# Attention followed by a gated token mixer on one core: TensorE's work regrouped into longer stretches of one kind, and its eight PSUM banks shared out anew

## The chip, the core and the metric

The kernel runs on one core of one Trainium2 chip. The metric is the device time of one execution in microseconds, of which three were taken before the change: 924.58, 922.16 and 916.06, with a median of 922.16. A lower time is better.

## What is computed

The reference has two parts. The first is attention with a sliding window, for 8 sequences of 576 tokens with 8 heads of 64 channels. The second is a token mixer on the 512 channels of all heads together. Cut to what matters:

```python
scores = scale * np.matmul(q, k.transpose(0, 1, 3, 2))          # (8, 8, 576, 576)
mask = (rel >= 0) & (rel < 128)                                  # rel = query - key
scores = np.where(mask, scores + slope[h] * -np.abs(rel), -1e9)
attn = softmax(scores)
x = heads_side_by_side(np.matmul(attn, v))                       # (8, 576, 512)

theta = x @ w_theta
zr, zi = x * np.cos(theta), x * np.sin(theta)
y = w_tok_r @ zr + w_tok_i @ zi                                  # mixes the tokens
u = x + y
out = u + np.maximum(u @ w_ch, 0.0)
```

## The kernel before

**Precision.** Most products are made of two or three TensorE products: an operand is split into a rounded high part and a remainder (the names end in h and l, or hi and lo), and high·high, high·low and low·high add up in one PSUM tile.

**Attention** works on pairs of heads (`Pair`, 32 of them, four for each sequence). A pair's scores come in three tiles, `scores((0, 2))`, `scores((3, 4))` and `scores((1,))` (line 271; the numbers are blocks of query rows). TensorE's part (line 285) is 12, 12 and 6 matmuls in which the two heads use 64 rows of the array each, so that two run side by side; they write one PSUM tile `s_ps` of two banks. VectorE adds the bias to it and takes the row's least value (line 292, 4, 4 and 2 times), which empties the tile into `s_sb`. ScalarE makes the exponential (line 296).

A head (`Head`, line 299) then goes through two steps per half, called bank 0 (query blocks 0, 2 and 1) and bank 1 (blocks 3 and 4). `flip(bank)` turns the exponentials over on TensorE (line 316, five or four transposes into one PSUM tile `t_ps`), and ScalarE and VectorE split the result into two fp16 parts `pt` (lines 362 and 363). `values(bank)` multiplies it with v (line 333, 15 and 12 products for the two banks, each 128x65 or 128x64 in fp16, into `acc`). `finish` (line 336) divides by the sum and writes the head's columns of `x_sb`.

**The mixer** follows for each sequence in three parts, written as generators whose parts can be taken one at a time. `turn` (line 366) goes over five blocks of tokens: `columns` transposes x (line 386), splits it and keeps a copy in `xtf` (lines 397 to 399). `products` multiplies with w_theta (line 406, 12 matmuls of 512 columns, 8 for the last block), and `angle` makes cosine and sine (lines 420 to 428), multiplies with x (430, 432) and splits the result into `z_hi` (line 377, ScalarE) and `z_lo` (line 378, GpSimd). `mix` (line 452) makes the eight pieces of y, each 27 matmuls of 288 columns (line 465), yielding after every three; VectorE adds the piece to `xtf` (line 470). `channels` (line 476) makes the last product, eight pieces of 12 matmuls (line 485) and the rectified sum (line 488). All PSUM tiles of the mixer come from one pool, under the name `mm`.

**What sets the order.** `attend` (line 518) runs the attention of sequence b+1 while `other`, the mixing of sequence b, is handed out in steps of three matmuls between its parts: 18 steps per pair, four pairs. The order in which `attend` calls things is only a first word, though. The program is then scheduled by priorities and a timeline of its own, which moves instructions on each engine; within an engine they run in the order that results. The first 96 us or so are `start` (line 561): the first sequence's attention, with the weights being unpacked beside it. After the last sequence's attention there is a mixer with no attention beside it.

**PSUM** has eight banks, shared among four pools (lines 63 to 66): `s_ps` two buffers of two banks each, `t_ps` one, `acc` one, `mm` two.

**Values.** `load_values` (line 189) fetches v of four heads and takes its largest absolute value on VectorE at once (line 197); `spread_scales` (line 202) makes a power of two of it.

Of the kernel before, what the change touches and what calls it, by code (L numbers as in the profile page):

```python
# [11 lines left out]
F32 = mybir.dt.float32  # L12
# [8 lines left out]
B, H, S, D = 8, 8, 576, 64  # L21
DM = H * D
NT = 5
# [13 lines left out]
GROUP = 4  # L37
# [9 lines left out]
def attn_moe_kernel(ctx: ExitStack, tc: tile.TileContext, qt, kt, vx, wth, wtok, wch, band, out):  # L47
    nc = tc.nc
    PSUM = bass.MemoryType.PSUM
# [5 lines left out]
    vbp = ctx.enter_context(tc.tile_pool(name="vbp", bufs=2))  # L55
# [4 lines left out]
    tp = ctx.enter_context(tc.tile_pool(name="tp", bufs=2))  # L60
    uf = ctx.enter_context(tc.tile_pool(name="uf", bufs=2))
    big = ctx.enter_context(tc.tile_pool(name="big", bufs=1))
    ps_s = ctx.enter_context(tc.tile_pool(name="ps_s", bufs=2, space=PSUM))
    ps_t = ctx.enter_context(tc.tile_pool(name="ps_t", bufs=1, space=PSUM))
    ps_a = ctx.enter_context(tc.tile_pool(name="ps_a", bufs=1, space=PSUM))
    ps_m = ctx.enter_context(tc.tile_pool(name="ps_m", bufs=2, space=PSUM))

    class Ring:

# [117 lines left out]
    group_v = {}  # L187

    def load_values(g):

        b, h = divmod(GROUP * g, H)
        vb = vbp.tile([128, GROUP, NT, 65], F32, name="vb")
        nc.sync.dma_start(out=vb, in_=vx[b, h:h + GROUP].rearrange("h p (c d) -> p h c d", d=65))
        most = rings["most"].take()
        nc.vector.tensor_reduce(out=most, in_=vb[:, :, :, :64], axis=mybir.AxisListType.XY, op=ALU.max,
                                apply_absolute_value=True)
        nc.vector.tensor_scalar(out=most, in0=most, scalar1=2.0 ** -100, scalar2=None, op0=ALU.max)
        group_v[g] = vb, most  # L200

    def spread_scales(g):
        vb, most = group_v[g]
        m_ps = ps_m.tile([128, 512], F32, name="mm")
        nc.tensor.transpose(m_ps[:GROUP, :128], most, ident)
        whole = rings["whole"].take()
        nc.vector.tensor_reduce(out=whole[:GROUP, :1], in_=m_ps[:GROUP, :128], axis=mybir.AxisListType.X, op=ALU.max)
        spread = rings["vs"].take()
        nc.vector.tensor_scalar(out=spread[:GROUP], in0=ident[:GROUP, :GROUP], scalar1=whole[:GROUP, :1],
                                scalar2=None, op0=ALU.mult)  # L210
        w_ps = ps_m.tile([128, 512], F32, name="mm")
        nc.tensor.matmul(w_ps[:, :GROUP], ones[:GROUP].broadcast_to([GROUP, 128]), spread[:GROUP],
                         start=True, stop=True)
        scale = rings["scale"].take()
        nc.vector.tensor_scalar(out=scale.bitcast(I32), in0=w_ps[:, :GROUP].bitcast(I32), scalar1=0x7F800000,
                                scalar2=None, op0=ALU.bitwise_and)
        nc.vector.tensor_scalar(out=scale.bitcast(I32), in0=scale.bitcast(I32), scalar1=-1.0,
                                scalar2=float((2 * 127 + VEXP) << 23), op0=ALU.mult, op1=ALU.add)
        group_v[g] = vb, scale
# [40 lines left out]
    class Pair:  # L260
# [10 lines left out]
        def scores(self, tiles, behind=None):  # L271

            ps = ps_s.tile([128, 2, 512], F32, name="s_ps")
            sbs = [sp.tile([128, len(tiles), 128 if tiles == (1,) else 256], F32, name=f"s_sb{len(tiles)}")
                   for _ in range(2)]
            if 0 in tiles:

                for sb in sbs:
                    nc.gpsimd.memset(sb[:64, 0, 192:], 0.0)  # L279
            for k, i in enumerate(tiles):  # L280
                q0, qn, k0, kn, c0 = TILES[i]
                for j, (qm, km) in enumerate(self.terms):
                    for e in range(2):
                        rows = slice(64 * e, 64 * e + 64)
                        nc.tensor.matmul(ps[:qn, e, 256 * k:256 * k + kn], qm[rows, q0:q0 + qn], km[rows, k0:k0 + kn],  # L285
                                         start=(j == 0), stop=(j == len(self.terms) - 1))
            for k, i in enumerate(tiles):
                _, qn, _, kn, c0 = TILES[i]
                for e in range(2):
                    sb = sbs[e][:qn, k, :kn]  # L290
                    least = self.mx[:qn, e, i:i + 1]
                    nc.vector.tensor_tensor_reduce(out=sb, in0=ps[:qn, e, 256 * k:256 * k + kn],  # L292
                                                   in1=bnd[:qn, c0:c0 + kn], scale=2.0 ** -((2 * self.p + e) % H + 1),
                                                   scalar=3.0e38, op0=ALU.add, op1=ALU.min, accum_out=least)
                    with tc.issue_after(behind.ins) if behind is not None else nullcontext():
                        self.exp = nc.scalar.activation(sb, sb, AF.Exp, bias=least, scale=-1.0)  # L296
                    self.heads[e].sc[i] = sbs[e][:qn, k]
# [196 lines left out]
    pairs = B * H // 2  # L494
# [9 lines left out]
    def step(stream, k=1):  # L504
        for _ in range(k):
            next(stream, None)
# [11 lines left out]
    def attend(b, x_sb, other, first, behind):  # L518

        for g in range(H // 2):  # L520
            p = b * H // 2 + g
            one, two = first.pop(0).heads
            new = None
            if p + DEPTH < pairs:
                new = Pair(p + DEPTH)
                first.append(new)

            def scores(tiles):
                if new is not None:
                    new.scores(tiles, behind)  # L530

            one.flip(0)
            step(other)
            scores((0, 2))
            step(other, 2)
            one.flip(1)
            step(other, 3)
            one.values(0)
            two.flip(0)
            step(other, 3)  # L540
            one.values(1)
            one.finish(x_sb)
            if new is not None:
                new.heads[0].ready()
            scores((3, 4))
            step(other)
            two.flip(1)
            step(other, 2)
            if p % 2 == 0 and p + 2 < pairs:
                spread_scales(p // 2 + 1)  # L550
            scores((1,))
            two.values(0)
            prepare(p + DEPTH + 2)
            step(other, 4)
            two.values(1)
            two.finish(x_sb)
            if new is not None:
                new.heads[1].ready()
            step(other, 2)

    def start(x_sb, load):

        paces = [0]

        def pace(k=1):
            for _ in range(k):
                paces[0] += 1
                if paces[0] * 3 % 5 < 3:
                    next(load, None)

        for p in range(2):
            prepare(p)
        last = None
        for p in range(H // 2 + 1):
            new = Pair(p) if p < H // 2 else None
            if new is not None:
                for head in new.heads:
                    head.ready()

            def scores(tiles):  # L580
                if new is not None:
                    new.scores(tiles)
                pace(2 * len(tiles))

            if last is not None:
                one, two = last.heads
                one.flip(0)
                one.flip(1)
                scores((0, 2))
                two.flip(0)  # L590
                one.values(0)
                one.values(1)
                one.finish(x_sb)
                scores((1,))
                two.flip(1)
                scores((3, 4))
                two.values(0)
                two.values(1)
                two.finish(x_sb)
            else:  # L600
                for tiles in SCORES:
                    scores(tiles)
            if new is not None:
                prepare(p + 2)
            last = new
        for _ in load:
            pass
# [31 lines left out]
    x_sb = xp.tile([128, NT, DM], F32, name="x_sb")  # L639
    start(x_sb, unpack(JOBS, ((big, "u_hi"), (big, "u_lo"), (uf, "xtf"), (uf, "xtf"))))  # L640
    for p in range(H // 2, H // 2 + DEPTH):
        load_values(p // 2)
        spread_scales(p // 2)
        first.append(Pair(p))
        for head in first[-1].heads:
            head.ready()
        for tiles in SCORES:
            first[-1].scores(tiles)
        prepare(p + 2)
    st[0]["exp"] = first[-1].exp  # L650
    rotated(turn(x_sb, st[0]), iter(()))
    for b in range(B):
        chans = urgent(channels(b, st[b]), CHAN if b else CHAN0)
        mixing = urgent(mix(st[b]), MIX if b else MIX0)
        other = ahead(mixing, chans) if b else ahead0(mixing, chans)
        if b + 1 < B:
            x_sb = xp.tile([128, NT, DM], F32, name="x_sb")
# [56 lines left out]
```

## Time and profile before

| | |
|---|---|
| median of three runs | 922.16 us |
| the profiled execution's own time | 919.67 us |
| its span, first to last instruction | 917.9 us |
| mean granted TensorE clock | 0.933 |
| TensorE busy (matmuls) | 797.7 us, 87% |
| VectorE, ScalarE, GpSimd busy | 62%, 53%, 29% |
| DMA | 49.65 MB, mean 54 GB/s |

The profile is of one execution. A group's row gives the busy time and the mean duration of one instruction. TensorE's matmuls are pipelined, so that the duration of one is longer than the time after which the next may start; what a matmul costs in a stream is the distance between the starts of two neighbours. An engine's instructions start in their order, so one that waits holds up all behind it. The order and the waits of one sequence's period come again in the next ones, so that one period of the middle can be read for all of them.

### The profile page before, as it was taken

The numbers are of one execution on the slowest core, as the hardware profiler recorded it, in microseconds if no ns is written. First come the engines' busy times: TensorE is split into PE (matmuls) and PEld (weight loads), VectorE is DVE, ScalarE is ACT, GpSimd is POOL, SyncE is SP. The second block draws the span as 40 slices with busy tenths as digits, with TensorE's granted clock in tenths as the row PEclk, the third lists the DMA queues.
The fourth block names the chain that finished last, engine by engine and source line by source line (L and its number), as shares of the span: only waits on it lengthen the run. The fifth ranks groups of instructions, "written<-read, shape, count | busy, mean of one in ns | idle before, by whom it ended". The sixth has DMA issues, their size and how long they took to land.

```text
span 917.9 us, 16440 instructions
## 1 busy us (share of the span) xinstructions
PE 797.7 (87%) x6338; PEld 694.8 (76%) x6338; DVE 566.7 (62%) x1535; ACT 488.2 (53%) x962; POOL 269.1 (29%) x324
## 2 busy tenths in 40 slices
PE   3669867999989888998889889898889988897898
PEld 3558656987878777887778778787678877796798
DVE  5897697565655765656755766556656567443522
ACT  5556467545664466544664456544674356632620
POOL 5773164211412233220422213121332105110331
PEclk9999886997989999999989989899989989798999
DMA  5541311021110210111110211112110210000001
GB/s 207 181 145 41 117 59 53 27 69 40 52 30 27 94 47 22 54 57 46 52 37 27 72 39 50 31 44 84 46 43 27 68 40 27 1 1 21 26 8 52
DMA packets 29550, 49.65 MB, mean 54 GB/s; under 512 B 2592, under 2 KB 19104, under 8 KB 29472
## 3 DMA queue, kind: packets, MB, share of 16 engines
q1 hardware_dynamic: 29472, 48.61, 16.5%
q8 instruction: 50, 0.82, 0.4%
q14 instruction: 28, 0.23, 0.1%
HBM read 39.16 MB, written 9.44 MB: 53 GB/s over the span
## 4 chain that ended last, share of the span: by engine, by line
PE 57%; DVE 16%; ACT 15%; DMA 6%; issue 3%; POOL 3%; ACTq 0%; SPq 0%; DVEq 0%; POOLq 0%
PE mm L465 20%; PE mm L406 10%; PE mm L485 8%; PE s_ps L285 6%; PE t_ps L316 6%; ACT s_sb L296 5%; PE acc L333 4%; DMA vb<-in_vx_dram 4%; DVE s_sb L292 2%; DVE g L423 2%; DVE f L421 2%; ACT z_hi L377 2%; ACT g L427 1%; DVE pt L363 1%; DMA xtf<-in_wch_dram 1%
## 5 line engine op out<-in xcount | busy, mean ns | idle before, releaser
L465 PE MATMUL mm<-wtk_hi,z_hi 128*128 128x288 f32 x576 | 180.4, 315 | 19.0 <-ACT z_hi L377 15.5
L465 PE MATMUL mm<-wtk_hi,z_lo 128*128 128x288 f32 x576 | 175.4, 311 | 0.6 <-POOL z_lo L378 0.4
L465 PE MATMUL mm<-wtk_lo,z_hi 128*128 128x288 f32 x576 | 174.9, 306 | 0.0
L292 DVE CUSTOM_DVE_ANT_0 s_sb<-s_ps,fixed 128x256 f32<-128x256 f32 (+2 forms) x320 | 108.5, 376 | 71.7 <-PE t_ps L316 63.7
L296 ACT ACTIVATE s_sb<-s_sb,fixed 128x256 f32<-128x256 f32 (+2 forms) x320 | 127.7, 465 | 14.0 <-DVE fixed L292 13.8
L465 PEld LDWEIGHTS mm<-wtk_hi,z_hi 128*128 128x128 f32 x576 | 111.4, 194 | 25.6 <-ACT z_hi L377 17.0
L316 PE MATMUL t_ps<-fixed,s_sb 128*128 128x128 f32 (+1 forms) x576 | 106.8, 304 | 24.9 <-DVE pt L363 9.2
L362 ACT ACTIVATE pt<-t_ps 128x512 f16<-128x512 f32 x112 | 66.8, 596 | 110.1 <-PE t_ps L316 109.3
L465 PEld LDWEIGHTS mm<-wtk_hi,z_lo 128*128 128x128 f32 x576 | 110.4, 194 | 5.1 <-POOL z_lo L378 3.5
L465 PEld LDWEIGHTS mm<-wtk_lo,z_hi 128*128 128x128 f32 x576 | 111.7, 194 | 1.5
L316 PEld LDWEIGHTS t_ps<-fixed,s_sb 128*128 128x128 f32 (+1 forms) x576 | 71.6, 156 | 40.5 <-ACT s_sb L296 10.8
L378 POOL TENSOR_TENSOR z_lo<-g,z_hi 128x512 fp32r<-128x512 f32 x40 | 53.0, 1326 | 140.0 <-ACT z_hi L377 140.0
L472 POOL TENSOR_TENSOR u_lo<-xtf,u_hi 128x288 fp32r<-128x288 f32 x64 | 53.6, 841 | 121.5 <-ACT u_hi L471 121.5
L333 PE MATMUL acc<-vh,pt 128*128 128x65 f16 x1008 | 82.4, 204 | 5.7 <-ACT pt L362 4.7
L333 PEld LDWEIGHTS <-pt 128*128 128x128 f16 x1512 | 70.7, 104 | 17.6 <-ACT pt L362 7.0
L363 DVE SCALAR_TENSOR_TENSOR pt<-t_ps,pt 128x512 f16<-128x512 f32 x112 | 76.2, 680 | 7.9 <-ACT pt L362 7.5
L285 PE MATMUL s_ps<-kh,qh 64*128 64x256 f32 (+2 forms) x320 | 61.8, 356 | 18.7 <-DVE fixed L292 10.8
L333 PE MATMUL acc<-vl,pt 128*128 128x64 f16 x504 | 70.5, 202 | 0.0
L285 PE MATMUL s_ps<-kh,ql 64*128 64x256 f32 (+2 forms) x320 | 55.8, 320 | 11.6 <-DVE ql L227 11.6
L230 POOL TENSOR_TENSOR kl<-kr,kh 128x576 fp32r<-128x576 f32 x32 | 49.1, 1535 | 56.5 <-ACT kh L229 51.2
L285 PEld LDWEIGHTS s_ps<-kh,qh 64*128 64x128 f32 (+1 forms) x320 | 35.7, 203 | 37.2 <-DVE fixed L292 14.6
L279 POOL MEMSET s_sb<- 64x64 f32 x64 | 9.1, 146 | 185.1 <-PE t_ps L316 185.1
(111 smaller groups left out, 1610.7 us busy)
## 6 DMA issues: line engine op xcount, KB each, us to landing
vb<-in_vx_dram SPq DMA_DIRECT2D x16, 650.0 KB, 4.3
qr<-in_qt_dram SPq DMA_DIRECT2D x32, 288.0 KB, 3.1
kr<-in_kt_dram SPq DMA_DIRECT2D x32, 288.0 KB, 2.9
out_dram<-xtf SPq DMA_DIRECT2D x64, 144.0 KB, 1.8
xtf<-in_wtok_dram SPq DMA_DIRECT2D x4, 576.0 KB, 4.6
xtf<-in_wch_dram SPq DMA_DIRECT2D x4, 512.0 KB, 3.8
u_hi<-in_wtok_dram SPq DMA_DIRECT2D x3, 576.0 KB, 3.9
u_lo<-in_wtok_dram SPq DMA_DIRECT2D x2, 576.0 KB, 5.0
```

Of the source, the lines that this page charges most:

```text
L285: nc.tensor.matmul(ps[:qn, e, 256 * k:256 * k + kn], qm[rows, q0:q0 + qn], km[rows, k0:k0 + kn], start=(j == 0), stop=(j == len(self.terms ...
L292: nc.vector.tensor_tensor_reduce(out=sb, in0=ps[:qn, e, 256 * k:256 * k + kn], in1=bnd[:qn, c0:c0 + kn], scale=2.0 ** -((2 * self.p + e) % ...
L296: self.exp = nc.scalar.activation(sb, sb, AF.Exp, bias=least, scale=-1.0)
L316: nc.tensor.transpose(t_ps[:, off:off + w], self.sc[i][:, 128 * j:128 * j + 128], ident[:w, :w])
L333: nc.tensor.matmul(av[:, i, :r.shape[-1]], l, r, start=(n == 0), stop=(n == len(prods) - 1))
L362: nc.scalar.activation(pt[:, 0], t_ps, AF.Copy, scale=2.0 ** PEXP)
L363: nc.vector.scalar_tensor_tensor(out=pt[:, 1], in0=t_ps, scalar=2.0 ** PEXP, in1=pt[:, 0], op0=ALU.mult, op1=ALU.subtract)
L378: nc.gpsimd.tensor_tensor(out=z_lo[:, c, :], in0=z, in1=z_hi[:, c, :].bitcast(F32), op=ALU.subtract)
L406: nc.tensor.matmul(t_ps, a[:, c * 128:c * 128 + 128], w[:, c, :], start=(k == 0 and c == 0), stop=(k == len(prods) - 1 and c == 3))
L465: nc.tensor.matmul(y_ps[:, :HALF], z[:, c, m * 128:m * 128 + 128], w[:, c, cs], start=(k == 0), stop=(k == 26))
L472: nc.gpsimd.tensor_tensor(out=u_lo[:, m, cs], in0=xtf[:, m, cs], in1=u_hi[:, m, cs].bitcast(F32), op=ALU.subtract)
L485: nc.tensor.matmul(o_ps[:, :HALF], w[:, c, e * 128:e * 128 + 128], u[:, c, cs], start=(k == 0), stop=(k == 11))
```

## The change

Four things are done.

1. In `attend`, both `flip` calls of a head stand together, both `values` calls of a head stand together, and the 18 mixing steps of a pair come as three parts of six instead of eight parts of one to four. `scores((1,))` moves behind the second head's `finish`.
2. The PSUM pools: `s_ps` goes from two buffers to one (four banks to two), `t_ps` from one to two, `mm` from two to three; `acc` keeps one. That is eight banks again.
3. `load_values` is cut in two: it only fetches, and the new `measure` takes the largest value later. `attend` calls `measure` in the second third of every other pair, and `spread_scales` later than before.
4. In `start`, one fetch of values is issued a pair earlier, since the pairs before the main loop need it measured.

```diff
-    ps_s = ctx.enter_context(tc.tile_pool(name="ps_s", bufs=2, space=PSUM))
-    ps_t = ctx.enter_context(tc.tile_pool(name="ps_t", bufs=1, space=PSUM))
+    ps_s = ctx.enter_context(tc.tile_pool(name="ps_s", bufs=1, space=PSUM))
+    ps_t = ctx.enter_context(tc.tile_pool(name="ps_t", bufs=2, space=PSUM))
     ps_a = ctx.enter_context(tc.tile_pool(name="ps_a", bufs=1, space=PSUM))
-    ps_m = ctx.enter_context(tc.tile_pool(name="ps_m", bufs=2, space=PSUM))
+    ps_m = ctx.enter_context(tc.tile_pool(name="ps_m", bufs=3, space=PSUM))
...
         nc.sync.dma_start(out=vb, in_=vx[b, h:h + GROUP].rearrange("h p (c d) -> p h c d", d=65))
+        group_v[g] = vb
+
+    def measure(g):
+        vb = group_v[g]
         most = rings["most"].take()
         nc.vector.tensor_reduce(out=most, in_=vb[:, :, :, :64], axis=mybir.AxisListType.XY, op=ALU.max,
...
             one.flip(0)
-            step(other)
+            one.flip(1)
             scores((0, 2))
-            step(other, 2)
-            one.flip(1)
-            step(other, 3)
+            step(other, 6)
             one.values(0)
-            two.flip(0)
-            step(other, 3)
             one.values(1)
             one.finish(x_sb)
             if new is not None:
                 new.heads[0].ready()
+            two.flip(0)
+            two.flip(1)
             scores((3, 4))
-            step(other)
-            two.flip(1)
-            step(other, 2)
+            if p % 2 == 0 and p + 2 < pairs:
+                measure(p // 2 + 1)
+            step(other, 6)
+            two.values(0)
+            two.values(1)
+            two.finish(x_sb)
+            scores((1,))
             if p % 2 == 0 and p + 2 < pairs:
                 spread_scales(p // 2 + 1)
-            scores((1,))
-            two.values(0)
             prepare(p + DEPTH + 2)
-            step(other, 4)
-            two.values(1)
-            two.finish(x_sb)
             if new is not None:
                 new.heads[1].ready()
-            step(other, 2)
+            step(other, 6)
...
+            if p == 3:
+                load_values(2)
...
-        load_values(p // 2)
+        measure(p // 2)
```

What the scheduler makes of it shows in the built programs. All lines from `measure` on stand four further down in the changed file (285 becomes 289, and so on). Taking a stretch to be TensorE instructions of one line in a row, the stretches are these:

| TensorE line (before) | instructions | stretches before | stretches after |
|---|---|---|---|
| 285, scores | 960 | 158, of which 38 hold a single matmul | 133, none of a single matmul |
| 316, transposes of a head | 576 | 138 | 141 |
| 333, products with v in fp16 | 1512 | 180, of which 7 hold a whole head's 27 | 87, of which 33 hold 27 |
| 465, mixing | 1728 | 151 | 151 |
| 485, channels | 768 | 63 | 81 |
| 406, angles | 448 | 40 | 45 |
| all lines | | 818 | 713 |

Two places show what the sums below rest on. The first is TensorE in the middle of the mixing, where a pair's last score tile, `scores((1,))`, is made. `s_ps` is its PSUM tile, `mm` is the mixer's, `t_ps` the transposes'. Before:

```order
L316 MATMUL t_ps<-fixed,s_sb_5394 128x128
L285 MATMUL s_ps<-kh,qh 128x128
L465 MATMUL mm<-wtk_hi,z_hi 128x288
L285 MATMUL s_ps<-kh,qh 128x128
L465 MATMUL mm<-wtk_lo,z_hi 128x288
L285 MATMUL s_ps<-kh,ql 128x128
L465 MATMUL mm<-wtk_hi,z_lo 128x288
L285 MATMUL s_ps<-kh,ql 128x128
L285 MATMUL s_ps<-kl,qh 128x128 x2
L465 MATMUL mm<-wtk_hi,z_hi 128x288
```

After the change, the same tile of a pair:

```order
L337 MATMUL acc<-vh,pt 128x65
L289 MATMUL s_ps<-kh,qh 128x128 x2
L289 MATMUL s_ps<-kh,ql 128x128 x2
L289 MATMUL s_ps<-kl,qh 128x128 x2
L216 MATMUL mm<-fixed 128x4
L320 MATMUL t_ps<-fixed,s_sb_5491 128x64 x2
L320 MATMUL t_ps<-fixed,s_sb_5491 128x128 x2
L469 MATMUL mm<-wtk_hi,z_lo 128x288
```

The two heads' matmuls stood apart with one mixing matmul between them; now they stand in pairs, and the tile is one stretch.

The second place is VectorE where it empties a tile `scores((0, 2))`, `s_ps`, into `s_sb` (each emptying has a second row that writes the least value to `fixed`). Before:

```order
L292 ISA s_sb_4995,fixed<-s_ps,fixed 64x192
L292 ISA fixed 64x1
L363 SCALAR_TENSOR_TENSOR pt<-t_ps,pt 128x512
L339 TENSOR_SCALAR fixed<-acc,fixed 128x5
L341 RECIPROCAL fixed<-fixed 128x5
L246 SCALAR_TENSOR_TENSOR vl<-vb,fixed,vh 128x320
L342 TENSOR_TENSOR x_sb<-acc,fixed 128x5x64
L292 ISA s_sb_4996,fixed<-s_ps,fixed 64x192
L292 ISA fixed 64x1
L292 ISA s_sb_4995,fixed<-s_ps,fixed 128x256
L292 ISA fixed 128x1
L292 ISA s_sb_4996,fixed<-s_ps,fixed 128x256
```

After the change, the same tile:

```order
L367 SCALAR_TENSOR_TENSOR pt<-t_ps,pt 128x512 x2
L296 ISA s_sb_4995,fixed<-s_ps,fixed 64x192
L296 ISA fixed 64x1
L296 ISA s_sb_4996,fixed<-s_ps,fixed 64x192
L296 ISA fixed 64x1
L296 ISA s_sb_4995,fixed<-s_ps,fixed 128x256
L296 ISA fixed 128x1
L296 ISA s_sb_4996,fixed<-s_ps,fixed 128x256
L296 ISA fixed 128x1
```

The emptying of a tile was spread around the work on a head's result; now its four parts stand in a row, behind the work on both of a head's transposed tiles.

## The prediction, made before the changed kernel ran

> **What bounds the kernel now.** I read the page first: busy times, and the chain that ended last.
>
> ```profile
> PE 797.7 (87%) x6338; PEld 694.8 (76%) x6338; DVE 566.7 (62%) x1535; ACT 488.2 (53%) x962; POOL 269.1 (29%) x324
> PE 57%; DVE 16%; ACT 15%; DMA 6%; issue 3%; POOL 3%; ACTq 0%; SPq 0%; DVEq 0%; POOLq 0%
> ```
>
> TensorE is the engine to look at, and the chain leaves it for VectorE and ScalarE in a third of the span: TensorE is short of time and also waits. Next, the stretches view, for one sequence's period in the middle (length, then busy time and count of TensorE, weight loads, VectorE, ScalarE, GpSimd, then the granted clock).
>
> ```profile
> 352.40:458.40 106.00, 95.83 (x803) 82.67 (x803) 66.46 (x186) 58.78 (x118) 26.50 (x38) 0.95 0.15 47
> ```
>
> A period is 106 us. Seven of them fill nearly all of the span behind the start. TensorE's 95.83 us busy isn't 95.83 us of use, since a matmul's duration contains its passage. So I read its timeline by the distance between starts.
>
> ```profile
> 400.83 0.29 PE L465 MATMUL mm<-wtk_hi,z_hi 128*128 128x288 f32 x1
> 400.96 0.29 PE L465 MATMUL mm<-wtk_lo,z_hi 128*128 128x288 f32 x1
> ...
> 401.17 0.38 PE L465 MATMUL mm<-wtk_hi,z_lo 128*128 128x288 f32 x1
> 401.39 0.29 PE L465 MATMUL mm<-wtk_hi,z_hi 128*128 128x288 f32 x1
> 401.61 0.33 PE L285 MATMUL s_ps<-kh,qh 64*128 64x128 f32 x2
> 401.78 0.27 PE L285 MATMUL s_ps<-kh,ql 64*128 64x128 f32 x2
> 401.89 0.28 PE L285 MATMUL s_ps<-kl,qh 64*128 64x128 f32 x1
> ...
> 402.17 0.19 PE L333 MATMUL acc<-vl,pt 128*128 128x64 f16 x1
> 402.20 0.22 PE L333 MATMUL acc<-vh,pt 128*128 128x65 f16 x2
> ...
> 402.50 0.81 PE L316 MATMUL t_ps<-fixed,s_sb 64*128 64x64 f32 x5
> 403.24 0.33 PE L285 MATMUL s_ps<-kl,qh 64*128 64x128 f32 x1
> 403.50 0.40 PE L465 MATMUL mm<-wtk_lo,z_hi 128*128 128x288 f32 x1
> 403.74 0.29 PE L465 MATMUL mm<-wtk_hi,z_lo 128*128 128x288 f32 x1
> ```
>
> In a stream a mixing matmul takes 0.13 us (400.83 to 400.96), a pair of scores 0.11 (401.78 to 401.89), a product with v 0.03 (402.17 to 402.20), five transposes 0.74. Leaving one kind for another costs on top. Behind two products with v, the first mixing matmul holds the next back to 0.22 us instead of 0.13 (401.17 to 401.39): 0.09. From mixing to scores it is 0.22 (401.39 to 401.61): 0.09 again. Behind scores the first mixing matmul takes 0.24 (403.50 to 403.74): 0.11. The dearest form is scores one at a time between mixing matmuls:
>
> ```profile
> 276.48 0.32 PE L285 MATMUL s_ps<-kh,qh 64*128 64x128 f32 x1
> 276.74 0.40 PE L465 MATMUL mm<-wtk_lo,z_hi 128*128 128x288 f32 x1
> 277.06 0.32 PE L285 MATMUL s_ps<-kh,qh 64*128 64x128 f32 x1
> ```
>
> One score and one mixing matmul take 0.58 us here (276.48 to 277.06); in streams they take half of 0.11 and 0.13, 0.19 together. Each single score wastes 0.39 us.
>
> Last, who waits for whom on TensorE, over the five periods from 247.4 to 777.3 us (total, times, longest):
>
> ```profile
> PE mm L465 <- ACT z_hi L377: 11.3, 5, 2.3
> PE mm L485 <- DVE f L421: 6.9, 9, 1.2
> PE s_ps L285 <- DVE ql L227: 6.2, 6, 1.2
> PE t_ps L316 <- ACT s_sb L296: 5.1, 5, 1.0
> PE t_ps L316 <- DVE pt L363: 3.8, 11, 0.6
> PE acc L333 <- ACT pt L362: 3.7, 5, 0.8
> PE s_ps L285 <- DVE fixed L292: 3.4, 13, 0.7
> PE mm L406 <- ACT xtf L394: 2.5, 4, 0.7
> PE mm L406 <- ACT xtf L399: 2.4, 3, 1.1
> PE mm L485 <- ACT xtf L399: 1.1, 5, 0.2
> ```
>
> That is 46.4 us, over 9 us a period, and no wait leads by far. Several are waits for a PSUM buffer rather than for data: lines 421, 394 and 399 are the last readers of an `mm` tile, 363 of `t_ps`, 292 of `s_ps`.
>
> **The change part by part.** (1) Fewer changes of kind. The 38 single scores become none: 38 x 0.39 = 14.8 us less. The other stretches of scores go from 120 to 133; one costs 0.09 to enter and some 0.2 to leave (0.11 and about 0.1 at its last pair), so 13 x 0.3 = 3.9 more. The counted orders have mixing behind products with v 56 times before and 13 now, 43 x 0.09 = 3.9 less; but mixing behind transposes 16 times before and 51 now. At the same 0.09, which I take since both are followed by the same matmul, that is 3.2 more. Channels and angles alternate more often (63 and 40 stretches become 81 and 45), with no price of its own in the rows above; from nothing to 2 us, I take 1 more. Sum: -14.8 + 3.9 - 3.9 + 3.2 + 1 = -11.6, call it **-11** (bounds -15 and -7). It lies on TensorE, with nothing beside it. The mixing is not in longer stretches at all, 151 before and after: the scheduler spends the parts of six again.
>
> The Trainium skill (TensorEngine Tiling (Array Packing), Key Properties) says that changing the tiling mode drains TensorE. By that rule only the 64-row scores would cost, 25 stretches fewer with two changes each at 0.09, 4.5 us, and the sum would come out 6.5 us later. The trace agrees at 401.61 and goes further: at 401.17 a change costs as much where both kinds use 128 rows.
>
> (2) Transposes ahead, two `t_ps`. With both flips of a head together and a second buffer, the transposes need not wait for line 363, and the products with v come a whole head behind the transposes, so that line 362 is done. The two rows are 3.8 + 3.7 = 7.5 us in five periods, 1.5 each, 10.5 in seven. I take **-9** (bounds -10.5 and -5). VectorE's and ScalarE's work for `pt` is the same; it is late for nobody, since other TensorE work stands between.
>
> (3) A third `mm` tile. The four rows of lines 421, 394 and 399 make 12.9 us in five periods, 18 in seven. A third buffer helps where the buffer is all that is missing; where the same ScalarE and VectorE work must deliver data next, the wait only moves. I take half, 9. The last mixer, without attention beside it, shows the wait alone (waits from 835 to 872 us, then TensorE's timeline):
>
> ```profile
> PE mm L485 <- DVE f L421: 3.5, 3, 1.4
> PE mm L485 <- ACT xtf L399: 1.8, 1, 1.8
> ```
>
> ```profile
> 849.70 0.80 PE L485 MATMUL mm<-u_hi,wch_hi 128*128 128x288 f32 x4 [0.97 <-DVE f L421]
> ```
>
> Channels, angles and transposes alternate there, with the same order after the change; with two tiles, the channels' tile is that of the angles before, still being read. The third removes that: 3.5 of the 5.3 us. Together **-12.5** (bounds -23 and -4).
>
> (4) Scores wait less for `ql`. Six waits, 6.2 us. In the new order two of a period's four such places have 25 mixing matmuls or a head's products behind the first two scores. Half of 8.7 in seven periods: **-4** (bounds -8.7 and 0).
>
> (5) One `s_ps`. The next tile's scores must now wait until VectorE has emptied the last one. In the trace of before, a tile's last scores and the emptyings that follow:
>
> ```profile
> 388.77 0.28 PE L285 MATMUL s_ps<-kl,qh 64*128 64x256 f32 x2
> ```
>
> ```profile
> 391.56 0.35 DVE L292 CUSTOM_DVE_ANT_0 s_sb<-s_ps,fixed 64x192 f32<-64x192 f32 x1 [2.44 <-PE t_ps L316]
> ...
> 397.24 0.46 DVE L470 TENSOR_TENSOR xtf<-mm,xtf 128x288 f32<-128x288 f32 x1 [3.20 <-PE mm L465]
> ...
> 398.38 0.41 DVE L292 CUSTOM_DVE_ANT_0 s_sb<-s_ps,fixed 128x256 f32<-128x256 f32 x1
> 398.72 0.68 DVE L363 SCALAR_TENSOR_TENSOR pt<-t_ps,pt 128x512 f16<-128x512 f32 x1
> ```
>
> Ten microseconds pass before the tile is empty, but VectorE idles for 5.64 of them: it waits in its own queue, first for transposes that free an `s_sb` buffer, then for a mixing piece. In the new order the transposes come first and the four emptyings stand in a row: 4 x 0.41 = 1.6 us, behind at most two `pt` of 0.68, so 3.0 us. Between two tiles TensorE now has, for example, 14 mixing matmuls, nine transposes and 27 products with v: 1.8 + 1.3 + 0.8 = 3.9 us. It fits on average, with 0.9 to spare. The old wait of 0.7 a period (3.4 in five) may go, or grow where `finish` or a mixing piece stands ahead: I take 1 us more a period, **+7** (bounds -5 and +20).
>
> (6) The start, where VectorE is nearly the bound (17.87 of 20 us):
>
> ```profile
> 40.00:60.00 20.00, 10.56 (x57) 9.15 (x57) 17.87 (x32) 9.64 (x18) 16.49 (x11) 1.00 0.55 170
> ```
>
> One `s_ps` lets less be made ahead of it, but TensorE has half of the time free: **+2** (bounds -3 and +8). Fetching values apart from measuring them takes a DMA wait from VectorE and moves no TensorE work; VectorE is not the bound there, so nothing. The wait of 11.3 us for `z_hi` stays, see the second rival.
>
> Sum: -11 - 9 - 12.5 - 4 + 7 + 2 = **-27.5 us** against the profiled execution's 919.67, so 892.2. That execution is 2.5 us below the median of the three runs (922.16); a median to be measured would be 894 to 895. I say **894**.
>
> **The rivals.** *A: the single score tile holds TensorE up.* If VectorE's own queue, without its idling, stays as long as in the rows above, a tile takes 10.0 - 5.6 = 4.4 us to empty. The shorter places between tiles hold 16 mixing matmuls, four transposes and 27 products with v, 2.1 + 0.6 + 0.8 = 3.5 us, so 0.9 us is missing. For the 56 large tiles of seven periods that is 50 us in place of the 7 above: -34.5 + 50 = +15.5, **938**, slower. It decides from 34.5/56 = 0.6 us a tile. For it: VectorE runs strictly in its order. Against it: the four emptyings stand together now. The Trainium skill speaks for this rival (Perfetto Trace Analysis, Matmuls): independent groups should rotate through different PSUM banks, so that emptying one overlaps the next one's matmuls. The change follows that for the mixer and drops it for the scores; the trace has not shown a single tile yet.
>
> *B: the saved waits come back at the next one.* The mixing's last products need `z_hi` of the last tokens, which stands on ScalarE behind 15 exponentials:
>
> ```profile
> 357.90 5.56 ACT L296 ACTIVATE s_sb<-s_sb,fixed 64x192 f32<-64x192 f32 x15
> ...
> 363.37 0.60 ACT L377 CAST z_hi<-g 128x512 fp32r<-128x512 f32 x1
> ```
>
> The new order still has 14 there. If the way through ScalarE and VectorE sets the period, what (2), (3) and (4) save is waited for there: -27.5 + 25.5 = -2, **920**. Against it: ScalarE is busy for 58.78 of 106 us.
>
> *C: the third tile gives all, and the clock with it.* The granted clock is 0.95 over a period; if the rest is at half speed, that is 10.6 us, which cost 5.3. Fewer waits could win half back, 18 us in seven periods, and the `mm` waits another 10.5: -27.5 - 28.5 = -56, **866**.
>
> **How the numbers follow.** My forecast has 0.55, with its own range 875 to 913; A 0.12, B 0.18, C 0.15. The range 864 to 924 takes in B, my own and most of C and leaves out A. A change of 1% is about what a measurement of this kernel can tell from none: 913 and 931 are the marks. Nearly all of my forecast and C are faster, 0.70; B is the same, 0.18; A slower, 0.12.
>
> **What would show it.** TensorE: single scores between mixing matmuls are gone; the waits of line 316 for 363 and of 333 for 362 are under 1 us a period; those for 421, 394 and 399 are about halved, and in the last mixer the 0.97 us is gone. The wait of the scores for the emptying (line 292, then 296) tells (5): under 2 us a period is my forecast, 6 or more is A. The wait for `z_hi` grown from 2.3 to 5 us or more a period is B. A granted clock of 0.97 in a period is C. A period of 102 us is right for the whole; 106 or more is wrong.

## The result: 803.8 us, and where 116 us went

The changed kernel takes 803.77 us (median of four runs, 802.54 to 803.89); the kernel before took 920.12 with a fourth run added. The ratio is 0.872, 95% interval 0.868 to 0.876. Faster was forecast, but 894 us, and the range ended at 864: the gain is four times the one predicted.

The profile after is read in the same order as the one before. First the page: busy times and the chain that ended last.

```profile
PE 740.5 (92%) x6338; PEld 656.0 (82%) x6338; DVE 567.2 (71%) x1535; ACT 481.8 (60%) x962; POOL 260.6 (32%) x324
PE 60%; DVE 16%; ACT 15%; issue 4%; DMA 3%; POOL 1%; SPq 0%; ACTq 0%; DVEq 0%; POOLq 0%
```

VectorE and ScalarE do the same work in nearly the same time as before (567 and 482 us). TensorE's 6338 matmuls are the same too, but it is busy 57 us less: the same matmuls then took less time each, or overlapped more. The clock line of the page stands in tenths for 40 slices; first before, then after.

```profile
PEclk9999886997989999999989989899989989798999
```

```profile
PEclk9999999799999999999999999999999999999999
```

Before, the granted clock fell twice in each of the five periods that the prediction read; after, it fell only between 138 and 162 us, around the beginning of the first mixing. The page's mean was 0.933 and is 0.991. The trace's clock record knows only full and half speed; half speed takes 124 us of it before, 2 x (1 - 0.9327) x 917.9, and 14 after. That leaves out the time ahead of the record, which comes below with the start.

Next the stretches: the five periods that the prediction read (530 us before), then one of them.

```profile
244.90:679.60 434.70, 430.86 (x4013) 384.70 (x4012) 325.68 (x931) 290.04 (x586) 131.93 (x186) 1.00 0.19 58
244.90:331.80 86.90, 85.95 (x804) 76.46 (x803) 66.51 (x186) 57.11 (x117) 25.88 (x37) 1.00 0.20 58
```

A period is 86.9 us instead of 106. TensorE is busy for all but 3.8 of 434.7 us, and the clock is 1.00 throughout. What is left of the waits in these five periods is the whole answer to that view:

```profile
PE acc L337 <- DVE pt L367: 1.4, 5, 0.5
PE t_ps L320 <- ACT s_sb L300: 1.1, 3, 0.4
PE mm L489 <- ACT xtf L403: 0.8, 4, 0.2
```

Before, ten rows made 46.4 us. The longest of them, 11.3 us for `z_hi`, is gone, and the scores no longer appear at all: not for `ql`, and not for the emptying of their single tile.

Of the 95.2 us that five periods lost, TensorE's idle time is 45.6 (49.5 to 3.8). The clock is 26: 58 us stood at half speed, 6 of them idle anyway, and half of the other 52 is an estimate of what full speed saves. Those 58 us are ten stretches. Five of 6.8 us begin while TensorE waits for the last `z_hi`; the other five, 24 us together, begin at the scores' wait of 1.1 to 1.2 us for `ql`. The remaining 23 us aren't divided up by any run. The changes of kind belong there, and the part of each wait that isn't shown as idle because the matmul before it is still passing (at 259.02 us before, 2.58 us between starts and 2.25 idle).

Of the whole 116 us, 95 come in these five periods, 12 in the one before them and 18 behind them; the start takes 9 more than before.

Why the wait for the last `z_hi` went shows in TensorE's and ScalarE's timelines at the start of a mixing:

```profile
338.10 0.29 PE L469 MATMUL mm<-wtk_hi,z_lo 128*128 128x288 f32 x1
...
341.28 0.38 PE L469 MATMUL mm<-wtk_hi,z_hi 128*128 128x288 f32 x1
...
344.51 0.29 PE L469 MATMUL mm<-wtk_hi,z_lo 128*128 128x288 f32 x1
344.64 0.29 PE L469 MATMUL mm<-wtk_hi,z_hi 128*128 128x288 f32 x1
```

```profile
338.13 5.28 ACT L300 ACTIVATE s_sb<-s_sb,fixed 64x192 f32<-64x192 f32 x14
343.31 0.60 ACT L381 CAST z_hi<-g 128x512 fp32r<-128x512 f32 x1
```

A piece of the mixing needs the last tokens' z only for its last three products. The 48th product, the last that two pieces can do without it, starts at 338.10. The third tile lets a third piece go on from 341.28, and its 24 products end with the one at 344.51. The `z_hi` cast, still behind 14 exponentials, is over at 343.91, and the first product that needs it starts at 344.64, without a wait.

The start went the other way: the first mixing begins at 145.0 us instead of 135.8. TensorE's longest waits up to there, before and after:

```profile
PE t_ps L316 <- ACT pt L352: 7.3, 3, 5.7
PE s_ps L285 <- ACT kh L229: 7.3, 1, 7.3
PE s_ps L285 <- DVE fixed L292: 7.2, 4, 3.9
```

```profile
PE s_ps L289 <- DVE fixed L296: 16.1, 5, 8.1
PE t_ps L320 <- ACT s_sb L300: 7.2, 4, 3.0
PE s_ps L289 <- ACT kh L233: 6.9, 1, 6.9
```

The single score tile is waited for 16.1 us here instead of 7.2. That isn't where the 9.2 us are, though, because other waits became shorter: TensorE's idle time up to the first mixing is 44.1 us before and 43.8 after. What differs is its pace. The clock record begins only at 80.9 us before and at 117.7 after, and the page counts the time ahead of it as full speed. TensorE ran at half pace there. After the change, four matmuls of `products` take 1.87 us from start to start at 113.16, and 1.02 at 119.90:

```profile
113.16 2.07 PE L410 MATMUL mm<-wth_hi,x_hi 128*128 128x512 f32 x4
115.03 1.91 PE L410 MATMUL mm<-wth_lo,x_hi 128*128 128x512 f32 x4
...
119.90 1.18 PE L410 MATMUL mm<-wth_hi,x_hi 128*128 128x512 f32 x4
120.92 1.08 PE L410 MATMUL mm<-wth_lo,x_hi 128*128 128x512 f32 x4
```

Before, the products with v of the start follow each other after 0.213 us up to 80.7 us and after 0.112 from 80.9 on. By the reckoning above, with the time ahead of the record taken as half speed, the clock costs the start 30 us before and 43 after, which is more than the 9.2. Why it comes up 37 us later isn't shown. One score tile alone doesn't do it: of the kernels below, the two with 1/1/1/3 begin the mixing at 132.8 and 132.5 us, earlier than the kernel before, with records from 101.8 and 101.6.

### The profile page after: what moved, and what is told of

Read it like the earlier page. It is cut to its first block, busy times and chain, and to the rows that moved or that the text cites. A ratio compares the mean times of both kernels' runs of the same rounds, so it can differ in the third digit from the quotient of the medians.

```text
span 802.0 us, 16393 instructions
## 1 busy us (share of the span) xinstructions
PE 740.5 (92%) x6338; PEld 656.0 (82%) x6338; DVE 567.2 (71%) x1535; ACT 481.8 (60%) x962; POOL 260.6 (32%) x324
## 4 chain that ended last, share of the span: by engine, by line
PE 60%; DVE 16%; ACT 15%; issue 4%; DMA 3%; POOL 1%; SPq 0%; ACTq 0%; DVEq 0%; POOLq 0%
PE mm L469 19%; PE mm L489 10%; PE mm L410 8%; PE t_ps L320 8%; PE s_ps L289 7%; PE acc L337 7%; ACT s_sb L300 5%; DVE f L425 2%; DVE s_sb L296 2%; ACT z_hi L381 2%; ACT g L431 2%; PE mm L390 2%; DVE pt L367 1%; DMA vb<-in_vx_dram 1%; ACT L431 1%
## 5 line engine op out<-in xcount | busy, mean ns | idle before, releaser
L469 PE MATMUL mm<-wtk_hi,z_hi 128*128 128x288 f32 x576 | 172.8, 305 | 0.3 <-DVE xtf L474 0.3
L469 PE MATMUL mm<-wtk_hi,z_lo 128*128 128x288 f32 x576 | 167.4, 301 | 0.0
L320 PEld LDWEIGHTS t_ps<-fixed,s_sb 128*128 128x128 f32 (+1 forms) x576 | 67.4, 150 | 27.5 <-ACT s_sb L300 12.3
L289 PE MATMUL s_ps<-kh,qh 64*128 64x256 f32 (+2 forms) x320 | 57.5, 343 | 26.8 <-DVE fixed L296 19.8
L366 ACT ACTIVATE pt<-t_ps 128x512 f16<-128x512 f32 x112 | 63.3, 594 | 24.4 <-PE t_ps L320 23.9
L337 PE MATMUL acc<-vh,pt 128*128 128x65 f16 x1008 | 61.2, 195 | 2.9 <-DVE pt L367 1.7
L337 PEld LDWEIGHTS <-pt 128*128 128x128 f16 x1512 | 52.8, 98 | 10.1 <-DVE pt L367 2.9
L289 PE MATMUL s_ps<-kh,ql 64*128 64x256 f32 (+2 forms) x320 | 50.8, 302 | 5.8 <-DVE ql L231 5.8
L337 PE MATMUL acc<-vl,pt 128*128 128x64 f16 x504 | 55.8, 193 | 0.0
L475 ACT CAST u_hi<-xtf 128x288 fp32r<-128x288 f32 x64 | 27.0, 430 | 44.5 <-DVE xtf L474 44.5
```

The lines of the kernel that those rows point to most:

```text
L320: nc.tensor.transpose(t_ps[:, off:off + w], self.sc[i][:, 128 * j:128 * j + 128], ident[:w, :w])
L337: nc.tensor.matmul(av[:, i, :r.shape[-1]], l, r, start=(n == 0), stop=(n == len(prods) - 1))
L366: nc.scalar.activation(pt[:, 0], t_ps, AF.Copy, scale=2.0 ** PEXP)
L469: nc.tensor.matmul(y_ps[:, :HALF], z[:, c, m * 128:m * 128 + 128], w[:, c, cs], start=(k == 0), stop=(k == 26))
```

## The experiments

Each kernel was scheduled anew, so its instructions move beyond the lines edited; the counts of stretches are given where they matter. The pools are written as score tile / transposes / acc / mixer: 2/1/1/2 before, 1/2/1/3 after. After the result there were two theories: the buffers do it, by removing waits that also let the clock fall; or the longer stretches do it.

**Pools alone and calls alone.** The first kernel is the one before with only the pools changed.

```diff
-    ps_s = ctx.enter_context(tc.tile_pool(name="ps_s", bufs=2, space=PSUM))
-    ps_t = ctx.enter_context(tc.tile_pool(name="ps_t", bufs=1, space=PSUM))
+    ps_s = ctx.enter_context(tc.tile_pool(name="ps_s", bufs=1, space=PSUM))
+    ps_t = ctx.enter_context(tc.tile_pool(name="ps_t", bufs=2, space=PSUM))
...
-    ps_m = ctx.enter_context(tc.tile_pool(name="ps_m", bufs=2, space=PSUM))
+    ps_m = ctx.enter_context(tc.tile_pool(name="ps_m", bufs=3, space=PSUM))
```

> The kernel before with nothing changed but the four PSUM pools (score tile once, transposes twice, acc once, mixer three times). Theory 1, the buffers do it: the third mixer tile covers the wait for z_hi and the second transposes' tile the waits at line 316 and 333, with that the half-speed clock goes; at least 80% of the 116 us come, 805 to 828 us, granted clock over 0.98. Theory 2, the order of calls does it (longer stretches, fewer changes of kind): under 40% come, 875 to 915 us, and the wait for z_hi of 2.2 us a period stays.

> The pools alone once more, timed. One look gave 811.13 us against 803.8 of the changed kernel. If the order of the calls is worth anything beside the pools, 808 to 814 us, that is some 7 us; if the one look was off, 802 to 806 us.

Measured: 811.13 us in one execution, then 811.18 (four runs, 810.11 to 811.80), ratio 0.880 (0.873 to 0.888). Of the 116 us, 109 come with three numbers, as theory 1 had it. Its waits over the five periods from 248.4 to 687 us are all of this:

```profile
PE t_ps L316 <- ACT s_sb L296: 1.0, 4, 0.4
PE acc L333 <- DVE pt L363: 0.5, 2, 0.2
```

The longer stretches come with the pools as well. Without a line of `attend` touched, whole heads of 27 products stand together 32 times (7 before, 33 in the changed kernel), and single scores fall from 38 to 5. The second kernel is the changed one with the old pools 2/1/1/2.

> The changed kernel with the four PSUM pools of before (score tile twice, transposes once, acc once, mixer twice). Theory 1: 895 to 925 us, waits for z_hi as before, clock 0.93 to 0.95. Theory 2: 805 to 845 us. Under both the number of score matmuls that stand alone is near that of before (29 against 38), so that fewer changes of kind can't bring more than some 10 us.

Measured: 932.73 us in one execution, beside 925.99 for the kernel before on the same chip. Theory 1 is the one that holds, though this is 8 us above its range. The order of the calls brings nothing by itself. With the new pools the two kernels lie 7.4 us apart, 811.2 and 803.8, and the intervals of their ratios just overlap. What the longer stretches bring isn't tested here, since with the old pools they don't come about (heads together 7 times, as before); the kernels with one transposes' tile below test it.

**Which buffer.** The changed kernel with one of them taken away, 1/2/1/2 and 1/1/1/3:

> The changed kernel with two mixer tiles in place of three (one PSUM bank lies idle). Theory 1 in its sharp form, the third mixer tile is the main thing: TensorE can make only two pieces' 24 products before it needs the last z_hi, so 3.1 us of cover are gone in each of seven periods and the half-speed clock comes back behind the wait: 22 us for the cover, up to 36 us for the clock, 840 to 865 us, clock under 0.97. If the second transposes' tile or the order is the main thing: 805 to 820 us, clock over 0.98.

> The changed kernel with one transposes' tile in place of two (one PSUM bank lies idle). If the second transposes' tile only removes the two waits of 1.5 us a period seen before: 814 to 825 us. If it is the main thing, because both flips of a head and what hangs on them can only then run ahead: over 850 us.

Measured: 891.41 us with two mixer tiles, granted clock 0.962, and 866.24 with one transposes' tile, clock 0.953, one execution each. The first is beyond both of its ranges; the second is in the range for the transposes' tile being worth far more than its two waits. With two mixer tiles, the waits of the whole span begin like this (then a period in the middle):

```profile
PE s_ps L289 <- DVE fixed L296: 16.4, 8, 8.1
PE mm L489 <- DVE f L425: 14.8, 15, 1.4
PE t_ps L320 <- ACT s_sb L300: 12.2, 12, 3.0
PE mm L469 <- ACT z_hi L381: 11.7, 6, 2.0
```

```profile
351.20:450.50 99.30, 91.66 (x803) 79.33 (x802) 64.97 (x186) 58.19 (x118) 26.41 (x38) 0.98 0.16 50
```

The wait for `z_hi` and the channels' wait for line 425 (421 before) are back, and the period is 99 us.

Then the same from the other side: the kernel before with one score tile and nothing else (1/1/1/2), with the third mixer tile besides (1/1/1/3), with the second transposes' tile besides (1/2/1/2), and the changed kernel with a fourth mixer tile in place of the second for transposes (1/1/1/4).

> The kernel before with one score tile in place of two and nothing else (two PSUM banks lie idle). This is the price of term 5 by itself. If the two buffers that the banks buy are worth what their absence cost the changed kernel (62 us for the transposes' tile, 88 for the mixer's), and these simply add, it must take 804 + 62 + 88 = 954 us. If the single score tile costs about the 7 us of the prediction, 915 to 935 us, and the two buffers together bring less than the sum of their absences, since either wait alone already lets the clock fall. Rival A of the prediction wanted 50 us.

> The kernel before with one score tile and three mixer tiles (transposes once; one bank lies idle). If the order of the calls in the source matters little, it takes what the changed kernel with one transposes' tile took, 866 us, within 15 us; waits for z_hi near nothing. If longer stretches matter beside the buffers: 880 us or more.

> The kernel before with one score tile and two transposes' tiles (mixer twice; one bank lies idle). If the order of the calls matters little: 891 us within 15 us, as the changed kernel with two mixer tiles; the wait for z_hi of 2 us a period stays and the clock is under 0.97. If the second transposes' tile brings only the 9 us of the prediction's second term: 905 to 925 us.

> The changed kernel with one transposes' tile and four mixer tiles (all eight banks in use). If mixer tiles are what counts, the fourth gives as much as the transposes' second did: 800 to 825 us. If the transposes' tile has a use of its own: it stays near the 866 us of three mixer tiles, 845 to 880 us.

| kernel | tiles | us | ratio to before |
|---|---|---|---|
| before | 2/1/1/2 | 920.1 | |
| before, score tile once | 1/1/1/2 | 913.9 | 0.991 (0.987 to 0.995) |
| before, transposes twice | 1/2/1/2 | 895.4 | 0.972 (0.960 to 0.984) |
| before, mixer three times | 1/1/1/3 | 850.8 | 0.924 (0.912 to 0.935) |
| changed, mixer four times | 1/1/1/4 | 850.5 | 0.923 (0.912 to 0.935) |
| before, both (pools alone) | 1/2/1/3 | 811.2 | 0.880 (0.873 to 0.888) |
| changed kernel | 1/2/1/3 | 803.8 | 0.872 (0.868 to 0.876) |

The single score tile costs nothing; it is 6 us faster. In its five periods from 250.6 to 769.8 us the scores wait 1.7 us for its emptying where they waited 3.4 for two tiles, and the mixing waits 9.8 us for `z_hi`, not much less than the 11.3 before:

```profile
PE mm L465 <- ACT z_hi L377: 9.8, 5, 2.0
...
PE s_ps L285 <- DVE fixed L292: 1.7, 10, 0.2
```

From there the second transposes' tile alone brings 18.5 us, the third mixer tile alone 63.1, and both together 102.7, which is 21 more than their sum. The page's mean clock in these four kernels is 0.934, 0.964, 0.964 and 0.984: while one cause of waits is left, the clock still falls for it. That doesn't make the 21 us, though. In five periods, the idle time falls by 12, 23 and 40 us with the transposes' tile, the mixer's and both, and the clock's loss by 21, 19 and 35, so neither falls by much more than the sum. What differs is the rest of TensorE's time, which grows by 20 us with the transposes' tile alone. In the order of the traces, 38 score matmuls stand alone there, against 12 with neither tile and 8 with both. At the prediction's 0.39 us each that is an estimated 10 us; the other half isn't explained.

The kernel with the third mixer tile and the old calls has the `z_hi` wait no more: it isn't among the waits of its five periods. A whole head's 27 products stand together only 3 times in its trace, so its 63 us don't come from longer stretches there. A fourth mixer tile brings the changed kernel with one transposes' tile 15.7 us (866.24, one execution, to 850.5), where a second transposes' tile in the same bank brings 62. The old calls with 1/1/1/3 take as little, 850.8, which is 15.5 us less than the changed calls with the same pools and just outside the 15 us that I had allowed. With equal pools, the order of the calls moves the time by 4 to 15 us, in either direction, in part by single executions. I had expected the absences to add up to a single score tile at 954 us, or 915 to 935; it was 913.9, just below the second.

**A wait and the clock.** The changed kernel, with ScalarE held up for the last tokens of each sequence:

```diff
                 nc.scalar.activation(g[:n], g[:n], AF.Sin, bias=halfpi[:n], scale=-RAD)
+            for _ in range(10 if i == 0 else 0):
+                nc.scalar.copy(g[:n], g[:n])
```

> The changed kernel with ten idle copies put on ScalarE behind the cosine of each sequence's last tokens, which make the last z some 6 us late and change nothing else in what is computed. It tests whether a wait on TensorE costs more than its own length through the clock. In the changed kernel the third piece's 24 products end at 344.5 us where the last z_hi is there at 343.9, so nearly all of the 6 us must show as a wait. A wait alone: at most 8 x 6 = 48 us more, 804 to 852 us, clock still over 0.98. With the clock: half-speed stretches of 6.8 us behind the wait come back in each period, clock under 0.965, and the time lost is the waits and 2 to 3.4 us more a period.

Measured: 890.03 us (889.66 to 890.40), clock 0.942. The clock line of its page, and a period in the middle:

```profile
PEclk9999998689996999989997999899998999799999
```

```profile
354.20:454.00 99.80, 91.95 (x804) 81.14 (x803) 65.28 (x188) 64.33 (x129) 25.74 (x38) 0.95 0.17 50
```

The clock falls in each period again. TensorE's idle time over the whole span rises from 61 to 113 us, 52 more, and the clock takes another 32 by the same reckoning as above (102 us of the record at half speed, 28 of them idle; in the changed kernel 14 and 3). Together they are 84 of the 86 us. The wait didn't come where I had put it: the scheduler planned around the late `z_hi`, single scores came back (23), and in five periods the longest waits are for a head's result and for the transposes' tile.

```profile
PE acc L337 <- DVE x_sb L346: 14.1, 5, 3.5
PE t_ps L320 <- DVE pt L367: 8.8, 5, 2.3
```

So this shows that idle time on TensorE costs more than its own length, by way of the clock; it doesn't isolate one wait.

**A better start.** The score tile is short only in the start, where no mixer tile exists yet. Its banks can serve as a second score tile there, and in a second kernel, which does the same with a pool `ps_y` of one bank, there is a second `acc` too. The first kernel's edit (its list `score_pools` begins with `ps_s`):

```diff
-            ps = ps_s.tile([128, 2, 512], F32, name="s_ps")
+            score_pools.append(score_pools.pop(0))
+            ps = score_pools[0].tile([128, 2, 512], F32, name="s_ps")
...
-    start(x_sb, unpack(JOBS, ((big, "u_hi"), (big, "u_lo"), (uf, "xtf"), (uf, "xtf"))))
+    with tc.tile_pool(name="ps_x", bufs=1, space=PSUM) as ps_x:
+        score_pools.append(ps_x)
+        start(x_sb, unpack(JOBS, ((big, "u_hi"), (big, "u_lo"), (uf, "xtf"), (uf, "xtf"))))
+        score_pools.remove(ps_x)
+    ps_m = ctx.enter_context(tc.tile_pool(name="ps_m", bufs=3, space=PSUM))
```

> The changed kernel with a second score tile during the first sequence's attention alone, where no mixer tile is in use yet (its banks go to the mixer afterwards). There the changed kernel waits 16.1 us for the emptying of the score tile against 7.2 before, and its first mixing starts 9.2 us later. If that wait is what the single tile costs: 8 to 10 us less than the changed kernel, 793 to 797 us. If VectorE's unpacking of the weights sets the start anyway: within 3 us of 804 us.

> As the kernel with two score tiles in the start, with the one bank that is still free there used as a second tile for the products with v. There TensorE waited 12.6 us for the result's reading before the next head's products. If that wait is on the way that ends the start: 786 to 794 us. If it only moves to VectorE, which unpacks the weights: within 3 us of 798 us.

Measured: 798.34 us (790.77 to 799.72, five runs), ratio 0.867 (0.863 to 0.870), with the second score tile; 793.11 (792.29 to 794.74, four runs), ratio 0.861 (0.855 to 0.867), with both. In the first, TensorE's longest waits up to the first mixing are these:

```profile
PE acc L338 <- DVE x_sb L347: 12.6, 3, 7.8
PE s_ps L290 <- ACT kh L233: 7.2, 1, 7.2
PE acc L338 <- ACT pt L357: 6.1, 2, 5.4
PE t_ps L321 <- ACT s_sb L301: 4.6, 3, 2.8
PE s_ps L290 <- DVE fixed L297: 3.6, 3, 2.1
```

The wait for the emptying went from 16.1 to 3.6 us, but the median fell by 5.4 us, not by 8 to 10, and the interval of its ratio overlaps the changed kernel's. These waits don't explain the sum. The traced execution is the shortest of the five, 790.77 us. Its first mixing begins at 131.9 us, 13 us earlier than in the changed kernel, and that is all of its gain. Its idle time up to there is 42.5 us against 43.8, but its clock record begins at 85.1 us instead of 117.7, and the clock costs its start an estimated 31 us instead of 43. When the clock first came up in the four longer executions isn't known. The second `acc` removes the wait for the result's reading, and waits for ScalarE's `qh`, `pt` and `kh` lead there in turn. The kernel with both is the fastest of all here, its ratio clear of the changed kernel's; whether it beats the one with the score tile alone is not settled, as their intervals overlap.

## Why the prediction was wrong, step by step

- **What bounds the kernel** was right: TensorE, short of time and waiting, with no single wait in the lead. All of these waits could go, though, and nothing else stood behind them: ScalarE is busy 57 of 86.9 us in the new period and VectorE 66.5.
- **(3), the third mixer tile, -12.5 us, is the step that failed.** The tile is worth 63 us on the kernel with one score tile, and 88 between the changed kernel and the one without it (one execution). The step halved the waits for buffers, on the ground that ScalarE and VectorE must deliver next; and the text kept the wait for `z_hi`, "the wait of 11.3 us for `z_hi` stays", because the exponentials ahead of it stayed. It did not ask what TensorE could do meanwhile: the third tile is also 24 more products that need no last z, 3.1 us of cover. The exponentials are still there, 14 of them, and the wait is gone; with the third tile alone and the old calls it is gone too.
- **The clock was left out of the sum.** It stood only in rival C, at half of what it could give, 18 us in seven periods. From the first mixing on, the reckoning above gives 47 us lost to half speed before and 3 after. This part became 125 us shorter; the clock is 44 of them, next to 58 of idle time (76 to 18 us). Both terms that remove waits, (3) and (4), had to be priced with the clock that the waits cost.
- **(2), transposes ahead, -9 us.** The mechanism was right: the waits of lines 316 and 333 for `pt` fell from 7.5 to 1.4 us in five periods. The size was off; alone, the second tile brings 18.5 us, clock included.
- **(4), the scores' wait for `ql`, -4 us:** all of it went, 6.2 us in five periods, which makes 8.7 in seven. The 24 us at half speed that began at these waits went with it, and the term had no price for them.
- **(5), one score tile, +7 us, had the wrong sign.** It takes 6 us less by itself. The reading that VectorE was late because it idled in its own queue fits what followed: with one tile the wait for the emptying fell. With it the score matmuls that stand alone fell from 39 to 12 in the order of the traces, which at 0.39 us each is more than the 6 us. Rival A, at 938 us, is ruled out in the periods.
- **(6), the start, +2 us,** was too little: the first mixing came 9.2 us later. The score tile was waited for longer, as the term had it, but the idle time didn't grow; the half-speed time did, and no term had that.
- **(1), fewer changes of kind, -11 us,** was not measured by itself, since the pools shorten the list of changes too. Its five parts add up to -10.6, not -11.6, which still rounds to -11. The single scores vanish as counted. The remainder of 23 us in five periods has room for it. Longer stretches aren't the main cause of the gain: the third mixer tile brings its 63 us without them, and idle time and clock make 72 of the 95 us in five periods.
- **Rival B** is ruled out: the waits of the periods fell from 46.4 to 3.3 us, and the one row that is new has 1.4. **Rival C** came nearest and pointed the right way, at 866 us, 62 above the result; it priced the waits for the mixer's tiles and the clock, and left the wait for `z_hi` standing like the forecast.

## What to carry to other kernels

Count the PSUM buffers before the order of the work: ask for each wait of TensorE not only what releases it, but how many more independent products it could start if it had one more tile. A wait on TensorE is priced at its length plus the half-speed time behind it: here, 3.4 to 6.8 us at half speed stood behind single waits of 1.2 us. Several causes of such waits had to go together before the clock stayed up. Before a mean clock is trusted, it must be known where the clock record begins. A buffer that looks doubled for a good reason may be the cheapest one to give away; try it by itself.

## What the runs showed of the hardware

The clock falls after far less than a full stop. In the kernel before, these are 3.4 us that end in the wait for `z_hi` and the 6.9 us behind them, then 3.4 us with the wait for `ql` and the 3.4 us behind them (TensorE's busy time comes first, the granted clock is the third number from the end):

```profile
255.00:258.40 3.40, 0.74 (x15) 0.43 (x11) 1.08 (x5) 3.40 (x11) 0.13 (x1) 1.00 0.00 0
258.40:265.30 6.90, 5.90 (x41) 4.91 (x42) 4.32 (x13) 4.88 (x12) 2.87 (x3) 0.51 0.32 96
```

```profile
313.05:316.46 3.41, 2.08 (x23) 1.41 (x23) 2.83 (x13) 2.29 (x4) 1.52 (x2) 1.00 0.01 2
316.46:319.87 3.41, 3.32 (x30) 2.97 (x30) 2.49 (x6) 1.45 (x3) 0.00 (x0) 0.50 0.56 173
```

TensorE was busy for 0.74 of 3.4 us in the first case, in 15 matmuls, and for 2.08 of 3.41 in the second. Both times the next stretch ran at half speed, although TensorE was busy for nearly all of it. There a mixing matmul follows its neighbour after 0.24 us (259.43 to 259.67) instead of 0.13.

The Trainium skill (TensorE: Matmul & The Clock Gate, HAM oscillation — how this bites in real kernels) names this mechanism, with gaps that cross a window of about 3.4 us. The traces agree on the length of the window: in all fourteen, every stretch of full or half speed is a multiple of 3.413 us, but for the last one, which the end of the record cuts. They also show that the gaps inside it (1.03 and 2.25 us in the first case, 1.17 in the second) need not fill it. Cut on this grid, the traces hold 128 falls. TensorE was busy for 10% to 72% of the window before a fall. Every window at full speed that was busy for less than 49% was followed by half speed, and none that was busy for more than 72%; in between both happened.
